# Attention scores of the first batch by single chunks on four row strips, in two lasting PSUM tiles, and the last stores on two queues

## Chip, cores, metric

One core of one Trainium2 chip. The metric is the device time of one execution in microseconds (us). The kernel before takes 404.97 us (median of 3 runs, 404.37 to 405.53). "Clock" below is the mean TensorE clock that was granted in a run, as a share of full speed.

## The reference

Attention over 8 batches of 12 heads (448 tokens, 64 wide), then a feed-forward layer with a SiLU gate on its result:

```python
def _attn_ref(q, k, v):                        # (8, 12, 448, 64) each
    scores = (1.0 / np.sqrt(64)) * np.matmul(q, k.transpose(0, 1, 3, 2))
    scores = scores - np.max(scores, axis=-1, keepdims=True)
    attn = np.exp(scores)
    attn = attn / (np.sum(attn, axis=-1, keepdims=True) + 1e-09)
    return np.matmul(attn, v)

def _moe_ref(x, w_in, w_out):                  # (3584, 768), (768, 2048), (2048, 768)
    h = x @ w_in
    g = h * (1.0 / (1.0 + np.exp(-h)))
    return g @ w_out
# ... x is the attention's result, heads side by side in each token's row
```

## The kernel before

The program is laid out by a small planner in Python that simulates the engines and emits each instruction when its inputs should be ready. Letters in the profile: **s** scores (TensorE), **E** their exponentials (ScalarE), **a** the sums and products with V (TensorE), **xT** the normalised attention, **h** the first feed-forward product, **th** its tanh, **G** the gated result (VectorE), **o** and **p** the second feed-forward product, **ost** results on their way out, **z** products of zeros whose only purpose is to keep TensorE going until the first h.

Batch 0 is cut into units of 224 queries (7 of the 14 blocks of 32), four heads and four chunks of keys each; the later batches have 448 queries. A score product has only 32 rows, and the program places the heads of a group in row strips of TensorE that work side by side: a group of eight products of 224 columns takes 0.60 us on two strips (kernel before, at 9.77 us). The program allots eight banks of PSUM (512 columns of FP32 each in its tiles): four for scores, four (tag "m") for everything else.

```python
def score_banks(n, w, ys):
    for y in ys:                               # y: heads 0,1 or heads 2,3
        pS_t[(n, w, y)] = ps.tile([128, 2, 512], FP32, name=f"s_{n}_{w}_{y}",
                                  tag="s", bufs=2)     # two banks per tile, two tiles

def per_burst(n):
    return 2 if units[n][0] == 0 else 1        # batch 0: two chunks to a tile

def scores(n, w, ys):
    score_banks(n, w, ys)
    for c in range(per_burst(n) * w, per_burst(n) * (w + 1)):
        for e in range(2):
            for y in ys:
                for h in (2 * y, 2 * y + 1):
                    score(pS_t[(n, w, y)], n, c, e, h, 0, rows_of(n, c) // 32, 0)

def expo(n, w, y):                             # ... one exponential per tile, 2 x 448 elements
    nc.scalar.activation(out=E[(n, w)][0:kr, 2*y : 2*y+2, 0:nk],
                         in_=pS_t[(n, w, y)][0:kr, :, 0:nk], func=AF.Exp, scale=attn_scale)
# ... in the planner
PACE = 3
s_ring = Ring(2)                               # free scores tiles
split = ((0,), (1,)) if ns[0] < 6 else ((0, 1),)   # batch 0: one tile (two heads) at a time
qk_seq += [(ns, c, ys) for c in range(NCH // per_burst(ns[0])) for ys in split]
# ... fill a gap of TensorE ahead of the first h; "wait" is the gap that the planner expects
n = max(1, int((wait - 0.06) / mm(128)))
od.on_pe(Op("PE", n * mm(128), lambda n=n: run_zeros(n)), "full")
# ... stores
eng = nc.scalar if w % 2 and 4 * qd + 4 == NT * B and i == j else nc.sync
```

The softmax here doesn't subtract the row's maximum and nothing guards it: scores larger than these inputs give would overflow.

## Time and profile before

| | before |
|---|---|
| time, median of 3 | 404.97 us |
| TensorE busy | 395.0 us of a span of 403.9 |
| ScalarE busy | 233.7 us |
| first s, first h, first s of batch 1 | 8.19, 23.66, 36.93 us |
| last product ends, last result ready, last store issued | 398.17, 398.76, 401.80 us |

Read the moments in the third row as follows: up to the first h the kernel waits for loads and exponentials, and TensorE's gaps are filled with z; from there TensorE is the bound (96% of the chain that ended last), so a delay of the first h reaches the end. Two groups of the page are needed for comparison: line, engine, operation, output and input, count, then busy time, mean ns of one, and the engine's idle time before them with what ended it.

```profile
L348 ACT ACTIVATE E<-s 128x896 f16<-128x896 f32 (+1 forms) x172 | 149.2, 915 | 48.8 <-PE s L311 47.5
L311 PE MATMUL s<-QT,KT 32*128 32x448 f16 (+4 forms) x864 | 56.4, 340 | 0.4 <-ACT E L348 0.4
```

TensorE's scores waited for ScalarE for 0.4 us in the whole run.

### The profile page before, as it was taken

Reading aid. Unit: us, or ns where it says so; the run is one execution under the profiler, and the core shown is the slowest. Engines: PE = TensorE matmul, PEld = TensorE weight load, DVE = VectorE, ACT = ScalarE, POOL = GpSimd, SP = SyncE. Lnnn points to the kernel's source line nnn. Section 1 sums busy time; section 2 is a strip of 40 time slices with the busy share of each in tenths; the row PEclk is TensorE's granted clock in tenths of the full one; section 3 lists DMA queues with packets and bytes.
Section 4 is the critical chain, followed back from the end, with each engine's and each line's share of the span. In section 5 each row is a group of like instructions: output and inputs, shape, how many; then the busy total and the mean of one; then the engine's idle time right before and its main releaser. Section 6 shows DMA issues by size and latency. Waiting matters only on the chain.

```text
span 403.9 us, 9442 instructions
## 1 busy us (share of the span) xinstructions
PE 395.0 (98%) x3767; PEld 203.7 (50%) x3767; DVE 299.3 (74%) x646; ACT 233.7 (58%) x360; POOL 95.9 (24%) x175
## 2 busy tenths in 40 slices
PE   8999999999999999999999999999999999999994
PEld 8676765444443444444445434444445444655562
DVE  2456686999979797696688578878697677674763
ACT  2887896696566866544961495664971573224410
POOL 6686383724003515120000630530000000000000
PEclk9999999999999999999999999999999999999999
DMA  7999999967014935392002782643001300131014
GB/s 106 158 151 206 204 136 213 200 94 116 2 39 99 173 56 71 64 177 56 0 2 58 123 142 44 92 81 68 0 21 47 94 0 2 35 81 44 2 49 107
DMA packets 38747, 34.43 MB, mean 85 GB/s; under 512 B 11952, under 2 KB 37936, under 8 KB 38704
## 3 DMA queue, kind: packets, MB, share of 16 engines
q0 software_dynamic: 27952, 22.82, 39.2%
q1 hardware_dynamic: 10560, 10.83, 10.4%
q8 instruction: 29, 0.48, 0.5%
q10 hardware_dynamic: 192, 0.20, 0.2%
q14 instruction: 14, 0.11, 0.1%
HBM read 45.61 MB, written 11.01 MB: 140 GB/s over the span
## 4 chain that ended last, share of the span: by engine, by line
PE 96%; DVE 1%; ACT 1%; issue 0%; ACTq 0%
PE h L446 37%; PE p L537 30%; PE s L311 12%; PE a L375 11%; PE o L551 3%; PE z L1148 2%; ACT E L348 1%; DVE T L359 1%; DVE rdn L424 0%; DVE ost L590 0%; DVE sT L415 0%; ACT ost L604 0%; DVE G L493 0%; DVE X L493 0%; DVE inv L421 0%
## 5 line engine op out<-in xcount | busy, mean ns | idle before, releaser
L348 ACT ACTIVATE E<-s 128x896 f16<-128x896 f32 (+1 forms) x172 | 149.2, 915 | 48.8 <-PE s L311 47.5
L446 PE MATMUL h<-xT,w_in_t 128*128 128x448 f16 (+1 forms) x864 | 157.8, 332 | 0.1
L446 PEld LDWEIGHTS <-w_in_t 128*128 128x128 f16 x864 | 79.2, 98 | 72.6 <-issue 19.4
L457 ACT ACTIVATE th<-h 128x448 f16<-128x448 f32 (+1 forms) x144 | 71.7, 505 | 58.1 <-PE h L446 53.5
L493 DVE SCALAR_TENSOR_TENSOR G<-th,h 128x448 f16<-128x448 f16 (+2 forms) x144 | 74.7, 532 | 35.2 <-ACT th L457 33.3
L250 POOL DMA_DIRECT2D V<-in_v_dram x88 | 48.6, 566 | 124.4 <-PE a L375 105.2
L311 PE MATMUL s<-QT,KT 32*128 32x448 f16 (+4 forms) x864 | 56.4, 340 | 0.4 <-ACT E L348 0.4
L537 PEld LDWEIGHTS <-G 128*128 128x128 f16 x384 | 36.7, 98 | 28.5 <-issue 4.6
L537 PEld LDWEIGHTS <-S 128*128 128x128 f16 x312 | 29.5, 98 | 22.8 <-issue 4.3
L375 PE MATMUL a<-E,V 128*32 128x448 f16 (+3 forms) x864 | 40.3, 334 | 0.5 <-issue 0.5
L537 PE MATMUL p<-D,G 128*128 128x384 f16 x208 | 37.8, 326 | 0.5 <-DVE sT L415 0.5
L537 PE MATMUL p<-w_out_t,S 128*128 128x384 f16 x208 | 36.8, 326 | 0.0
L432 DVE SCALAR_TENSOR_TENSOR xT<-a,rdn 128x448 f16<-128x448 f32 (+1 forms) x54 | 28.7, 560 | 6.7 <-PE a L375 6.2
L537 PE MATMUL p<-w_out_t,G 128*128 128x384 f16 x176 | 31.8, 326 | 0.0
L311 PEld LDWEIGHTS <-KT 32*128 32x128 f16 (+2 forms) x864 | 17.5, 98 | 27.9 <-issue 26.6
L359 DVE TENSOR_TENSOR T<-E,E 128x1792 f16<-128x1792 f16 x20 | 21.7, 1086 | 11.4 <-ACT E L348 11.4
L375 PEld LDWEIGHTS <-V 128*32 128x32 f16 (+2 forms) x864 | 18.2, 95 | 22.9 <-issue 15.3
L527 DVE TENSOR_TENSOR S<-G 128x512 f16<-128x512 f16 x70 | 26.5, 417 | 4.3 <-PE p L537 4.2
L359 DVE TENSOR_TENSOR T<-T,E 128x1792 f16<-128x1792 f16 x20 | 21.7, 1085 | 8.8 <-ACT E L348 8.8
L231 POOL DMA_DIRECT2D rk<-in_k_dram x24 | 13.7, 570 | 41.4 <-DVE KT L285 38.0
L285 DVE STREAM_TRANSPOSE KT<-rk 128x256 f32<-128x256 f32 (+3 forms) x48 | 16.6, 383 | 7.9 <-DMA rk<-in_k_dram 6.9
L600 ACT COPY ost<-p 128x384 f32<-128x384 f32 x13 | 6.3, 482 | 24.4 <-PE p L537 24.4
(41 smaller groups left out, 270.5 us busy)
## 6 DMA issues: line engine op xcount, KB each, us to landing
out_dram<-ost SPq DMA_DIRECT2D x220, 48.0 KB, 1.6
rk<-in_k_dram POOLq DMA_DIRECT2D x24, 224.0 KB, 5.1
rq<-in_q_dram POOLq DMA_DIRECT2D x21, 224.0 KB, 5.7
w_out_t<-in_moe_w_out_dram POOLq DMA_DIRECT2D x8, 384.0 KB, 8.9
V<-in_v_dram POOLq DMA_DIRECT2D x43, 64.0 KB, 4.5
V<-in_v_dram POOLq DMA_DIRECT2D x40, 48.0 KB, 4.2
w_in_t<-in_moe_w_in_dram POOLq DMA_DIRECT2D x16, 96.0 KB, 4.5
w_in_t<-in_moe_w_in_dram POOLq DMA_DIRECT2D x8, 192.0 KB, 7.9
```

The costliest lines, as they stand in the source:

```text
L250: nc.gpsimd.dma_start(out=VT[b][32 * x : 32 * (x + 1), hs, 0:count, :], in_=v[b, hs].rearrange("h (i g) d -> i h g d", g=TPP)[:, :, first ...
L285: nc.vector.transpose(out=turned.rearrange("p c x i -> p x c i")[:, x:y, 0:count], in_=t[:, first : first + count * (y - x)].rearrange("p ...
L311: nc.tensor.matmul(out=pS[p0 : p0 + 32 * (x1 - x0), h % 2, at : at + nq], lhsT=KT[(b, hg)][32 * h : 32 * (h + 1), c, x0:x1, :, e], rhs=QT[ ...
L348: nc.scalar.activation(out=E[(n, w)][0:kr, 2 * y : 2 * y + 2, 0:nk], in_=pS_t[(n, w, y)][0:kr, :, 0:nk], func=AF.Exp, scale=attn_scale,)
L359: nc.vector.tensor_tensor(out=T_t[n], in0=E[(n, 0)] if c == 1 else T_t[n], in1=E[(n, c)], op=ALU.add,)
L375: nc.tensor.matmul(out=a[32 * h : 32 * (h + 1), 0:nq], lhsT=w, rhs=e[k0:k1, h, at : at + nq], start=start, stop=stop,)
L432: nc.vector.scalar_tensor_tensor(out=xT[(b, cc)][:, 32 * g0 : 32 * g1], in0=acc[(n, part)][:, 0:nq], scalar=0.5, in1=rdn_t[n].rearrange("p ...
L446: nc.tensor.matmul(out=h[:, 0 : t1 - t0], lhsT=w_in_t[:, cc, 128 * f : 128 * (f + 1)], rhs=xT[(b, cc)][:, t0:t1], start=(cc == 0), stop=(c ...
L457: nc.scalar.activation(out=th, in_=h_t[(b, f, t0)][:, 0 : t1 - t0], func=AF.Tanh)
L493: nc.vector.scalar_tensor_tensor(out=dst[:, f, at + lo : at + hi], in0=th_t[(b, f, t0)][:, lo - t0 : hi - t0], scalar=1.0, in1=h_t[(b, f, ...
L527: nc.vector.tensor_tensor(out=dst[:, f0:f1], in0=x[:, f0:f1], in1=y[:, f0:f1], op=op)
L537: nc.tensor.matmul(out=pr_t[(qd, BANK[m])][:, 0:OH], lhsT=w[:, f, :], rhs=W_[m][:, f, :], start=(f == 0 and BANK[m] == m), stop=(f == HF - 1),
```

## The change

Intent: batch 0's score groups use all four row strips, chunk by chunk, and two tiles that last over the whole batch take the chunks alternately in their left and right column halves, so that one half can be read while the other is written. The planner is told that the halves are free of each other. With it come a new pace of the score groups and new priorities, and the last four outputs all use both store queues.

```diff
-    def score_banks(n, w, ys):
+    def score_banks(n, c, ys):
         for y in ys:
-            pS_t[(n, w, y)] = ps.tile([128, 2, 512], FP32, ..., tag="s", bufs=2)
+            key = y if units[n][0] == 0 else (n, c, y)
+            if key not in pS_t:
+                pS_t[key] = ps.tile([128, 2, 512], FP32, ..., tag="s", bufs=2)
+            pS_t[(n, c, y)] = pS_t[key]
 ...
-        for c in range(per_burst(n) * w, per_burst(n) * (w + 1)):
-            for e in range(2): ...
+        for e in range(2): ...               # one chunk; at = nq * (c % 2) picks the half
 ...
-            in_=pS_t[(n, w, y)][0:kr, :, 0:nk],
+            in_=pS_t[(n, c, y)][0:kr, :, at : at + nq],
 ...
-    s_ring = Ring(2)
+    s_ring = (Ring(2), Ring(2))              # one ring per half
 ...
-            split = ((0,), (1,)) if ns[0] < 6 else ((0, 1),)
-            qk_seq += [(ns, c, ys) for c in range(NCH // per_burst(ns[0])) for ys in split]
+            qk_seq += [(ns, c, (0, 1)) for c in range(NCH)]
 ...
-            eng = nc.scalar if w % 2 and 4 * qd + 4 == NT * B and i == j else nc.sync
+            eng = nc.scalar if w % 2 and 4 * qd + 4 == NT * B else nc.sync
 ...
-    PACE = 3
+    PACE = 3.8
 # priorities (bias): tanh -2 to -0.3, gate -1 to -4, combine_w 100 to 30, reads of results
 # -0.3/-1 to 0.5/0, add_e 0 to 2, inverse -10 to 0, norm -10 to -2; limits: od.now - 4 to
 # od.now - 2, len(moe) < 6 to len(moe) < 24
 # (cut: the same renaming from per_burst to per_tile elsewhere)
```

More of the change, by code (lines that the diff above doesn't have):

```diff
@@ L299, in turn_q @@
         QT[n] = qt
-    def score_banks(n, w, ys):
+    def score_banks(n, c, ys):
         for y in ys:
-            pS_t[(n, w, y)] = ps.tile(
-                [128, 2, 512], FP32, name=f"s_{n}_{w}_{y}", tag="s", bufs=2
-            )
+            key = y if units[n][0] == 0 else (n, c, y)
+            if key not in pS_t:
+                pS_t[key] = ps.tile([128, 2, 512], FP32, name=f"s_{n}_{c}_{y}", tag="s", bufs=2)
+            pS_t[(n, c, y)] = pS_t[key]
     def score(pS, n, c, e, h, x0, x1, p0):
@@ L309, in score @@
         nq = 32 * (g1 - g0)
-        at = nq * (c % per_burst(n))
+        at = nq * (c % per_tile(n))
         nc.tensor.matmul(
@@ L317, in score, with per_tile, scores @@
         )
-    def per_burst(n):
+    def per_tile(n):
         return 2 if units[n][0] == 0 else 1
-    def scores(n, w, ys):
-        score_banks(n, w, ys)
-        for c in range(per_burst(n) * w, per_burst(n) * (w + 1)):
-            for e in range(2):
-                for y in ys:
-                    for h in (2 * y, 2 * y + 1):
-                        score(pS_t[(n, w, y)], n, c, e, h, 0, rows_of(n, c) // 32, 0)
+    def scores(n, c, ys):
+        score_banks(n, c, ys)
+        for e in range(2):
+            for y in ys:
+                for h in (2 * y, 2 * y + 1):
+                    score(pS_t[(n, c, y)], n, c, e, h, 0, rows_of(n, c) // 32, 0)
     def scores_rest(n):
@@ L341, in rows_of, with expo @@
         return KROWS[c] if form(*units[n][:2]) == "lone" else 128
-    def expo(n, w, y):
-        kr = rows_of(n, w * per_burst(n))
-        nk = 32 * (units[n][3] - units[n][2]) * per_burst(n)
+    def expo(n, c, y):
+        kr = rows_of(n, c)
+        nq = 32 * (units[n][3] - units[n][2])
+        w, at = c // per_tile(n), nq * (c % per_tile(n))
         if (n, w) not in E:
@@ L348, in expo @@
         nc.scalar.activation(
-            out=E[(n, w)][0:kr, 2 * y : 2 * y + 2, 0:nk],
-            in_=pS_t[(n, w, y)][0:kr, :, 0:nk],
+            out=E[(n, w)][0:kr, 2 * y : 2 * y + 2, at : at + nq],
+            in_=pS_t[(n, c, y)][0:kr, :, at : at + nq],
             func=AF.Exp,
@@ L369, in attend_mm @@
         nq = 32 * (g1 - g0)
-        at = nq * (c % per_burst(n))
+        at = nq * (c % per_tile(n))
         if part == 0:
@@ L396, in attend @@
                     attend_mm(
-                        a, n, part, c, h, 0, rows_of(n, c), E[(n, c // per_burst(n))],
+                        a, n, part, c, h, 0, rows_of(n, c), E[(n, c // per_tile(n))],
                         c == 0, lone and c == NCH - 1,
@@ L631 @@
     od = Order()
-    s_ring, m_ring, e_ring = Ring(2), Ring(4), Ring(NE)
+    s_ring, m_ring, e_ring = (Ring(2), Ring(2)), Ring(4), Ring(NE)
     th_ring, tmp_ring, ost_ring = Ring(3), {3: Ring(2), 1: Ring(1)}, Ring(NOST)
@@ L750, in run @@
                 th = od.add(
-                    Op("ACT", act(t1 - t0), lambda: tanh(b, f, t0, t1), [op], -2, tail=0.2, ring=th_ring)
+                    Op("ACT", act(t1 - t0), lambda: tanh(b, f, t0, t1), [op], -0.3, tail=0.2, ring=th_ring)
                 )
@@ L757, in run @@
                     [th],
-                    -1,
+                    -4,
                     then=lambda at: (m_ring.give(at), th_ring.give(at)),
@@ L789, in sums_w @@
                         ld_wout[0] + ld_wout[1] + list(plain_op.values()) * (m in (3, 7)),
-                        100,
+                        30,
                     )
@@ L807, in run @@
                     [op],
-                    -0.3,
+                    0.5,
                     then=lambda at: (m_ring.give(at), ost_ring.give(at + STORED)),
@@ L864, in read @@
             busy = act(OH) if eng == "ACT" else OH / 960.0 + 0.13
-            bias = -0.3 if eng == "ACT" else -1
+            bias = 0.5 if eng == "ACT" else 0
             ring = tmp_ring[m] if m in tmp_ring else ost_ring if m in (2, 5, 6, 7) else None
@@ L985, in qk_at, with halves_of @@
         at = when([kt_op.get(units[n][:2]) for n in ns] + [qt_op.get(n) for n in ns])
-        s, e = s_ring.when(len(ys)), (e_ring.when(1) if ys[0] == 0 else 0.0)
-        if at is None or s is None or e is None:
-            return None
-        return max(at, s, e)
+        s = [r.when(len(ys)) for r in halves_of(n, c)]
+        e = e_ring.when(1) if c % per_tile(n) == 0 and ys[0] == 0 else 0.0
+        if at is None or None in s or e is None:
+            return None
+        return max(at, e, *s)
+    def halves_of(n, c):
+        return s_ring[c % 2 : c % 2 + 1] if units[n][0] == 0 else s_ring
     def run_qk():
@@ L994, in run_qk @@
         nq = 32 * (units[n][3] - units[n][2])
-        s_ring.take(len(ys))
-        if ys[0] == 0:
+        halves = halves_of(n, c)
+        for r in halves:
+            r.take(len(ys))
+        if c % per_tile(n) == 0 and ys[0] == 0:
             e_ring.take()
@@ L1000, in run_qk @@
             "PE",
-            2 * per_burst(n) * mm(nq) + (0.03 if rest else 0.013),
+            2 * mm(nq) + (0.03 if rest else 0.013),
             (lambda: scores_rest(n)) if rest else (lambda: scores(n, c, ys)),
@@ L1005, in run_qk @@
         op.half = len(ys) == 1
-        if c == NCH // per_burst(n) - 1 and ys[-1] == 1:
+        if c == NCH - 1 and ys[-1] == 1:
             done = []
@@ L1017, in run_qk @@
                     "ACT",
-                    act(2 * nq * per_burst(n)),
+                    act(2 * nq),
                     lambda y=y: expo(n, c, y),
@@ L1021, in run_qk @@
                     tail=0.2,
-                    then=s_ring.give,
+                    then=lambda at: [r.give(at) for r in halves],
                 )
@@ L1039, in plan_e @@
             t_op[n] = [
-                od.add(Op("DVE", HG * S / 1920.0 + 0.1, lambda n=n, c=c: add_e(n, c), deps, 0))
+                od.add(Op("DVE", HG * S / 1920.0 + 0.1, lambda n=n, c=c: add_e(n, c), deps, 2))
             ]
@@ L1060, in av_at @@
         for n in ns:
-            if len(exp_op.get(n, ())) < 2 * NCH // per_burst(n):
+            if len(exp_op.get(n, ())) < 2 * NCH:
                 return None
@@ L1064, in av_at @@
             for i, x in enumerate(exp_op[n]):
-                c = i // 2 * per_burst(n)
+                c = i // 2
                 if len(ns) == 2 and c == NCH - 1:
@@ L1096, in then @@
             def then(at):
-                for _ in range(7 if two else NCH // per_burst(ns[0])):
+                for _ in range(7 if two else NCH // per_tile(ns[0])):
                     e_ring.give(at)
@@ L1119, in after_av @@
                     made[-1:] + before[step],
-                    -10,
+                    0,
                 )
@@ L1131, in after_av @@
                 [op] + rdn_op[n],
-                -10,
+                -2,
                 then=m_ring.give,
@@ L1167 @@
             if qk is not None and qk <= od.now and (
-                od.now >= pace["next"] or moe_i is None or len(moe) < 6
+                od.now >= pace["next"] or moe_i is None or len(moe) < 24
             ):
                 u0 = units[qk_seq[0][0][0]]
-                pace["next"] = min(max(pace["next"], od.now - 4), od.now) + PACE * len(qk_seq[0][2]) / 2
+                pace["next"] = min(max(pace["next"], od.now - 2), od.now) + PACE * len(qk_seq[0][2]) / 2
                 run_qk()
```

## The prediction

> **What bounds the kernel now.** I read the page first (busy time, clock row, chain), then TensorE's waits, then the timeline of the first 45 us and of the last 20.
>
> ```profile
> PE 395.0 (98%) x3767; PEld 203.7 (50%) x3767; DVE 299.3 (74%) x646; ACT 233.7 (58%) x360; POOL 95.9 (24%) x175
> ...
> PEclk9999999999999999999999999999999999999999
> ...
> PE 96%; DVE 1%; ACT 1%; issue 0%; ACTq 0%
> ```
>
> TensorE is busy throughout at full clock and is 96% of the chain. Its own list of waits is nearly empty:
>
> ```profile
> PE z L1148 <- DVE zeros L214: 1.0, 1, 1.0
> PE a L375 <- ACT E L348: 0.6, 1, 0.6
> PE p L537 <- DVE sT L415: 0.5, 1, 0.5
> PE a L375 <- issue: 0.5, 1, 0.5
> PE s L311 <- ACT E L348: 0.4, 1, 0.4
> ```
>
> But busy is not useful everywhere: until the first h, TensorE fills gaps with products of zeros (z). The timeline of the start and of the first scores of batch 1:
>
> ```profile
> 8.19 0.60 PE L311 MATMUL s<-QT,KT 32*128 32x224 f16 x16
> ...
> 8.80 4.14 ACT L348 ACTIVATE E<-s 128x896 f16<-128x896 f32 x5 [6.78 <-PE s L311]
> ...
> 9.77 0.60 PE L311 MATMUL s<-QT,KT 32*96 32x224 f16 x8 [0.43 <-ACT E L348]
> ...
> 23.66 0.74 PE L446 MATMUL h<-xT,w_in_t 128*128 128x224 f16 x6
> ...
> 36.93 0.58 PE L311 MATMUL s<-QT,KT 32*128 32x448 f16 x8
> ...
> 37.54 1.73 ACT L348 ACTIVATE E<-s 128x896 f16<-128x896 f32 x2 [0.96 <-PE s L311]
> ```
>
> So there are two regimes. From 8.2 to 23.66 the exponentials on ScalarE pace the kernel: five stand back to back in 4.14 us, a step of (4.14-0.915)/4 = 0.81 us each. From 23.66 on TensorE does, and everything that delays the first h delays the end. The end is a third regime, stores:
>
> ```profile
> 385.71 16.09 SPq L585 DMA_DIRECT2D out_dram<-ost  x28
> ...
> 397.98 1.82 ACTq L585 DMA_DIRECT2D out_dram<-ost  x4
> 398.20 0.56 DVE L590 TENSOR_TENSOR ost<-p,s 128x384 f32<-128x384 f32 x1 [0.26 <-PE p L537]
> ```
>
> The last result is ready at 398.76, but SyncE's queue still works through its stores to 385.71+16.09 = 401.80; the span ends 2.1 us later.
>
> [...]
>
> **The change part by part.**
>
> *Scores of batch 0.* Both kernels issue 24 groups of 8 products of 224 columns. Before, a group is two chunks of two heads, two row strips at a time: [...]the timeline has 0.50 to 0.53 from such a group to the next. After, it is one chunk of four heads on four strips[...]. [...]17 of the 24 groups stand before the first h (16 before the change), where TensorE waits anyway.
>
> *Exponentials of batch 0.* 24 of 896 elements become 48 of 448. Steps of 0.81 us at 896 and 0.237 at 224 (tanh) give about 0.43 at 448, so 0.85 for a pair: only 0.05 us more per chunk.
>
> *The banks.* This is where I choose. The four scores banks now belong to two tiles that last over the batch, and chunks alternate between their column halves. The kernel's own planner counts the halves as free of each other. The waits in the built program say otherwise[...]. In unit 0, the third chunk's first product waits for the exponential of chunk 2, heads 0 and 1, which reads the other half; the exponential of chunk 2, heads 2 and 3, waits for the third chunk's last product; and so on through the batch. Elsewhere the products wait for both exponentials of the chunk just before. Two engines that had two buffers now take turns. One turn:
> - two exponentials, the first 0.43 to the next's start, the second to its end 0.546 (the tanh row of that size): 0.97;
> - from an exponential's end to the waiting product: 0.05 (9.72 to 9.77 before);
> - from the first product to the start of the exponential: at 36.93/37.54, 0.61 us[...].
>
> Sum 1.45 us per chunk, against 0.81 for the same elements before. The first exponential still starts at 8.80. The third chunk's products come at 8.80 + 2x0.43 + 0.546 + 0.05 = 10.25, the seventeenth 14 turns later at 30.55, and the first h follows 0.32 us on, at **30.9 instead of 23.66: +7.2 us**. V's arrival (16.7), which held a 0.46 us wait before, no longer matters.
>
> From there to batch 1's first scores I walked the two engines through the remaining 7 chunks, the 7 h and the products with V in the built order. [...]the turns go on: with one h (0.56 us) between two chunks TensorE is back before the exponential is done, waits of 0.44, 0.55, 0.39, 0.3 and 0.65 us, 2.3 in sum. Before, this stretch had 1.0 in all, mostly the 0.6 of the list. Batch 1's scores come at about 43.5 instead of 36.93; one h fewer is done by then (0.56) and 16 products with V more (0.19), so the lag is **+6.9 us**. Everything after is TensorE's work without slack, so this lag reaches the end.
>
> *Pace and priorities.* The work from there is the same. Counting changes of mode in the built order: 180 against 185, -0.6 us. Waits left there in the trace before, as excess over the usual steps, add to about 4 us; the new order may gain or lose part of them, which I put at zero.
>
> *Stores.* Four of the 20 stores that SyncE issues after 392.2 go to ScalarE: 4 x 0.48 = 1.9 us off the backlog. The last pair of each queue can start only after 398.76 and needs some 0.9, so both queues end near 399.9, with a little for waits between stores: **-1.8 us**.
>
> Sum: 404.97 + 6.9 - 0.6 - 1.8 = **409.5 us**, 1.1% slower.
>
> **Rivals.**
> 1. *The turns cost nothing, the halves work as planned.* Then chunks flow at 0.85 us, the first h comes about 1 us earlier, 1.7 us are saved after it and 1.8 at the end: about 400.5. For it: the change was built around that; the kernel before shows five exponentials without a gap. Against it: the waits are in the built program, one engine's product on the other's exponential in every chunk, and no other work is there to fill the gaps.
> 2. *The turns cost more*, because the idle turns make TensorE's clock drop, or because a turn has hand-over times that I read too short. At half the clock a chunk gains 0.19 us and everything near it doubles: 3 to 4 us more, 413. For it: in each turn TensorE streams scores for 0.19 us and zeros for about 0.3 of 1.45 us.[...]
> 3. *The new order of the rest takes back the loss.* At most the 4 us of leftover waits: 405.5. It can also lose some: the normalisations and reads of results lose priority on VectorE, and later x or late banks would stall TensorE.
>
> **Range and chances.** The turn time carries the sum: 0.1 us per turn is 1.4 us at the first h. With plus or minus 1.5 us for that, 2 for the order of the rest and 0.5 for the end, 8 in 10 is **405.5 to 413.0**. Faster by over 2% would be below 396.9, which even rival 1 does not reach: 0.01. Slower by over 2% is above 413.1 and needs rival 2 or a bad order: 0.09. Within 2%: 0.90.
>
> **What would show it right or wrong.** In the timeline after: exponentials of 448 elements in pairs with idle time of about 0.5 us after every second, ended by PE s; the third chunk's products near 10.25; first h near 30.9 (rival 1: about 22.7); batch 1's first scores near 43.5. In the waits: PE s waiting for ACT E, several times with about 2 us in all after the first h. In the groups: exponentials of 448 at about 0.55 each. At the end: before, the last store's issue ends 3.0 us after the last result is ready (398.76 to 401.80); I expect 1.1 to 1.3, on both queues. If the first h is near 23 the lockstep is refuted; if it is near 31 and the total is below 405, the later order gained what I put at zero.

The sum came to 409.5 us, as printed; these of its terms lost their figures:

- The streaming times of a score group on two strips and on four are cut, and with them the third term of the turn, put at 0.43 us, and the 1.7 us that TensorE was to save from the first h to batch 1's scores. By the traces, a group on four strips takes 0.41 us and one on two 0.60, which is 0.19 less. With that, the third term is 0.61 - 0.19 = 0.42 us and the turn 0.97 + 0.05 + 0.42 = 1.44. Products of h of 224 columns follow each other at 0.097 us (trace before); an estimate from that for the saving, 8 x 4 x 0.097 - 7 x 2 x 0.097, is again 1.7 us.
- The cost of a change of mode (the next products are of another shape), from which the -0.6 us for five changes fewer comes, is cut. In the trace before, six products of h take 0.67 us from their start to the scores' (23.66 to 24.33), twelve 1.25 (27.82 to 29.07): 0.097 us each and 0.09 for the change, so five changes would be 0.45 us.
- The 0.48 us of a store, from one issue to the next, stood in a cut paragraph and is read from the trace before: there SyncE's issues in the backlog start 0.36 to 0.52 us apart, 0.46 in the mean (eight from 392.21 to 395.87).

One h (0.56 us) is 0.58 us by the same lines of the trace; 16 products with V (0.19) are 0.39 (32 take 0.96 us, 16 take 0.57); with both, the lag of 6.9 us would be 6.8.

## The result, and the profile after

The changed kernel takes **415.62 us** (median of 4 runs: 415.48, 414.11, 415.76, 416.03; clock 0.977 to 0.985), against 405.08 (4 runs) for the kernel before in the same rounds: **ratio 1.0255, 95% interval 1.0225 to 1.0285, slower**. A ratio here is the mean time of one kernel's fast runs over that of the other's fast runs of the same rounds, so it is not quite the ratio of the quoted medians. "Fast" means within 1.5% of the kernel's own fastest run. A kernel that loses clock in every run has only such runs, so I give the clock beside the times.

Parts 1, 2 and 5 of the page of the kernel after (busy times; the granted clock in 40 slices of 10.3 us, in tenths; the same two groups as before):

```profile
PE 399.8 (97%) x3794; PEld 205.7 (50%) x3794; DVE 299.9 (73%) x646; ACT 237.1 (57%) x384; POOL 95.8 (23%) x175
...
PEclk9578999999999999999999999999999999999998
...
L350 ACT ACTIVATE E<-s 128x896 f16<-128x896 f32 (+3 forms) x196 | 150.9, 822 | 58.5 <-PE s L312 57.8
...
L312 PE MATMUL s<-QT,KT 32*128 32x448 f16 (+4 forms) x864 | 55.6, 350 | 6.8 <-ACT E L350 6.2
```

Work barely changed: 1.7 us more on ScalarE for 24 more exponentials, 0.8 us less on scores. Three other things did. Scores wait for E 6.2 us instead of 0.4; ScalarE sits idle before its exponentials 58.5 us instead of 48.8; and the clock row, 9s throughout before, has a dip to 5, 7 and 8 in its second to fourth slices.

The timeline of the kernel after, first turns (start, duration, engine, instruction, count, idle time before it and what ended that):

```profile
8.05 1.42 ACT L350 ACTIVATE E<-s 128x448 f16<-128x448 f32 x3 [6.03 <-PE s L312]
9.51 0.41 PE L312 MATMUL s<-QT,KT 32*96 32x224 f16 x8 [0.78 <-ACT E L350]
9.85 0.51 PE L1155 MATMUL z<-zeros 128*128 128x128 f16 x6
9.97 0.97 ACT L350 ACTIVATE E<-s 128x448 f16<-128x448 f32 x2 [0.50 <-PE s L312]
10.99 0.41 PE L312 MATMUL s<-QT,KT 32*96 32x224 f16 x8 [0.63 <-ACT E L350]
...
16.11 0.61 PE L312 MATMUL s<-QT,KT 32*96 32x224 f16 x8 [0.75 <-ACT E L350]
...
17.80 0.61 PE L312 MATMUL s<-QT,KT 32*96 32x224 f16 x8 [0.32 <-ACT E L350]
...
32.84 1.30 PE L448 MATMUL h<-xT,w_in_t 128*128 128x224 f16 x6
...
46.31 0.57 PE L312 MATMUL s<-QT,KT 32*128 32x448 f16 x8
```

TensorE and ScalarE take turns: each score group waits for an exponential, each pair of exponentials waits for a score group. A turn lasts 10.99 - 9.51 = 1.48 us, later 17.80 - 16.11 = 1.69. The later turns are longer because TensorE's part is: 0.61 us for the same eight products instead of 0.41. The windows of both kernels (length, busy time and count of PE, PEld, DVE, ACT, POOL, then the granted clock, DMA share, GB/s), before first:

```profile
10.00:15.00 5.00, 5.00 (x82) 3.33 (x79) 2.15 (x6) 4.78 (x7) 2.38 (x5) 1.00 1.30 160
```

after:

```profile
10.00:15.00 5.00, 3.74 (x58) 2.12 (x57) 1.52 (x4) 2.88 (x6) 2.87 (x6) 0.72 1.29 160
15.00:20.00 5.00, 3.72 (x44) 2.35 (x41) 0.62 (x3) 2.92 (x6) 4.50 (x9) 0.50 1.19 186
20.00:25.00 5.00, 5.00 (x93) 3.12 (x93) 2.45 (x7) 3.10 (x7) 3.86 (x7) 0.50 0.99 149
```

From about 12 us to about 26 TensorE ran at half clock, and for a few us more between 30 and 40 (0.77 and 0.89 in the windows 30 to 35 and 35 to 40). Everything on the way to the first h is affected. Note that "PE busy" is 5.00 in the last window although the engine runs at half speed: the busy column alone hides this, the clock column shows it.

Cutting both profiled runs at the same five moments shows where the time went. "Again" is the same changed kernel; the last two columns are experiments described below (both at a clock of 0.998 in these runs):

| stretch, us | before | after | after, again | more zeros | turns alone |
|---|---|---|---|---|---|
| start to first s | 8.19 | 7.44 | 8.15 | 7.28 | 7.32 |
| first s to first h | 15.47 | 25.40 | 22.50 | 22.90 | 22.92 |
| first h to first s of batch 1 | 13.27 | 13.47 | 13.57 | 12.95 | 12.91 |
| from there to the last product's end | 361.24 | 362.56 | 362.56 | 362.55 | 362.28 |
| from there to the end of the span | 5.76 | 4.84 | 4.99 | 4.05 | 3.93 |
| span | 403.93 | 413.71 | 411.77 | 409.73 | 409.36 |

The first row is not the change's doing: over all profiled runs of all variants it lies between 6.67 and 8.19. The second row carries +9.9 us, the fourth +1.3, the fifth -0.9.

### The profile page after: what moved, and what is told of

Same layout as the page of the kernel before. It is cut to its first block, busy times and chain, and to the rows that moved or that the text cites. A ratio compares the mean times of both kernels' runs of the same rounds, so it can differ in the third digit from the quotient of the medians.

```text
span 413.7 us, 9524 instructions
## 1 busy us (share of the span) xinstructions
PE 399.8 (97%) x3794; PEld 205.7 (50%) x3794; DVE 299.9 (73%) x646; ACT 237.1 (57%) x384; POOL 95.8 (23%) x175
## 4 chain that ended last, share of the span: by engine, by line
PE 93%; ACT 4%; DVE 1%; issue 0%
PE h L448 36%; PE p L539 29%; PE a L377 12%; PE s L312 12%; ACT E L350 4%; PE o L553 3%; PE z L1155 2%; DVE G L495 0%; DVE T L361 0%; DVE QT L296 0%; DVE ost L592 0%; ACT th L459 0%; DVE inv L423 0%; DVE zeros L214 0%; DVE ones L212 0%
## 5 line engine op out<-in xcount | busy, mean ns | idle before, releaser
L350 ACT ACTIVATE E<-s 128x896 f16<-128x896 f32 (+3 forms) x196 | 150.9, 822 | 58.5 <-PE s L312 57.8
L448 PEld LDWEIGHTS <-w_in_t 128*128 128x128 f16 x864 | 80.6, 98 | 70.3 <-issue 15.1
L377 PE MATMUL a<-E,V 128*32 128x448 f16 (+3 forms) x864 | 42.6, 346 | 0.7 <-DVE G L495 0.7
L539 PEld LDWEIGHTS <-S 128*128 128x128 f16 x312 | 29.4, 98 | 22.9 <-issue 4.5
L312 PEld LDWEIGHTS <-KT 32*128 32x128 f16 (+2 forms) x864 | 15.4, 100 | 35.5 <-issue 33.0
L377 PEld LDWEIGHTS <-V 128*32 128x32 f16 (+2 forms) x864 | 19.2, 99 | 24.3 <-issue 16.3
L417 DVE STREAM_TRANSPOSE sT<-a 128x448 f32<-128x448 f32 (+1 forms) x27 | 15.7, 582 | 11.3 <-PE a L377 10.7
```

What stands on the lines that cost most here:

```text
L312: nc.tensor.matmul(out=pS[p0 : p0 + 32 * (x1 - x0), h % 2, at : at + nq], lhsT=KT[(b, hg)][32 * h : 32 * (h + 1), c, x0:x1, :, e], rhs=QT[ ...
L350: nc.scalar.activation(out=E[(n, w)][0:kr, 2 * y : 2 * y + 2, at : at + nq], in_=pS_t[(n, c, y)][0:kr, :, at : at + nq], func=AF.Exp, scal ...
L377: nc.tensor.matmul(out=a[32 * h : 32 * (h + 1), 0:nq], lhsT=w, rhs=e[k0:k1, h, at : at + nq], start=start, stop=stop,)
L448: nc.tensor.matmul(out=h[:, 0 : t1 - t0], lhsT=w_in_t[:, cc, 128 * f : 128 * (f + 1)], rhs=xT[(b, cc)][:, t0:t1], start=(cc == 0), stop=(c ...
L539: nc.tensor.matmul(out=pr_t[(qd, BANK[m])][:, 0:OH], lhsT=w[:, f, :], rhs=W_[m][:, f, :], start=(f == 0 and BANK[m] == m), stop=(f == HF - 1),
```

## The experiments

Each is built from one of the two kernels. All gave results that agree with the reference. The first four ran on one chip, beside ten runs of the kernel before (median 405.27; two of the ten were slow: 410.93 and 411.09, clock 0.986 and 0.977).

### Old scores, everything else new

The kernel after, with batch 0's scores as before (the score hunks and `s_ring` of the diff undone).

> The changed kernel with batch 0's scores, exponentials and scores tiles as before (two chunks of two heads, 24 exponentials of 896); pace, priorities and stores stay changed. If the lasting, shared banks cost the time (theory A), the first h is back near 23.7 us, the clock stays full and the total is within 2 us of the kernel before less the 0.9 us at the end: 402 to 406 us. If pace and priorities cost it (theory B), the first h may be near 23.7 but the total stays above 410.

Measured: 404.99 us, **ratio 0.9993** (0.9979 to 1.0008), clock 0.998 to 1.000; first h at 22.94. So the loss is in the scores: without them pace, priorities and stores together change nothing.

### The scores alone

The kernel before with only the score hunks and `s_ring` of the diff.

> The kernel before with only the scores of batch 0 changed; pace, priorities and stores of before. Theory A: first h near 32 to 33 us as in the changed kernel, total 413 to 418. Theory B (pace and priorities): close to 405.

Measured: 415.72 us, **ratio 1.0271** (1.0243 to 1.0299), clock 0.975 to 0.987; first h at 32.56. The scores' change alone gives the whole loss, 10.5 us.

### The stores alone

```diff
-            eng = nc.scalar if w % 2 and 4 * qd + 4 == NT * B and i == j else nc.sync
+            eng = nc.scalar if w % 2 and 4 * qd + 4 == NT * B else nc.sync
```

> The kernel before with only the stores of the last four outputs on two queues. My prediction's term: 1.8 us less (403.2). The trace of the changed kernel, whose end after the last product is 4.84 us against 5.76, says 0.9 us less (404.1). If the end is bound by the last transfers and not by the queue, no change.

Measured: 403.27 us, **ratio 0.9948** (0.9934 to 0.9962), five of the six runs between 403.08 and 403.33. This is the best kernel and beats both, by 2.0 us and 12. From the last result to the end of the last store's issue it takes 1.3 us, 3.04 before. Its profile fell in its one disturbed run (408.10 us, clock 0.987), which is read only for that end.

The three results also show what pace and priorities cost by themselves: old scores, with them, 404.99; stores alone, without them, 403.27. That is **+1.7 us**.

### More zeros in each gap

The kernel after, its order untouched, with six more products of zeros in the first filled gap after each score group (210 instead of 138). This tests whether the clock, not the turns, made the difference between 409.5 and 415.6.

```diff
     def scores(n, c, ys):
+        warm["s"] = 1
 ...
-        for _ in range(n):
+        for _ in range(n + 6 * warm.pop("s", 0)):
             nc.tensor.matmul(out=warm["z"][:, 0:128], lhsT=zeros, rhs=zeros, ...)
```

> The changed kernel with six more products of zeros (0.33 us) in each of the gaps that zeros fill in the first 33 us, the order otherwise the same. If the halved clock between about 12 and 26 us adds to the turns (theory C), the granted clock stays at 1.00 there, a turn goes from 1.65 to 1.47 us, and the first h comes 1.5 to 2.5 us earlier, near 30.7; total 412 to 414. If the zeros delay the scores, or the clock falls all the same, no gain or a loss.

Measured: 411.65 us, **ratio 1.0162** (1.0147 to 1.0177), clock 0.995 to 0.998. Timeline and one of the windows of this kernel:

```profile
9.36 0.41 PE L314 MATMUL s<-QT,KT 32*96 32x224 f16 x8 [0.45 <-ACT E L353]
9.69 0.84 PE L1156 MATMUL z<-zeros 128*128 128x128 f16 x12
10.83 0.41 PE L314 MATMUL s<-QT,KT 32*96 32x224 f16 x8 [0.29 <-ACT E L353]
```

```profile
15.00:20.00 5.00, 4.17 (x78) 3.10 (x78) 0.15 (x2) 3.51 (x8) 4.46 (x8) 1.00 1.21 191
```

A turn is still 10.83 - 9.36 = 1.47 us, but the clock stays at 1.00 and no turn grows. Adding work to TensorE made the kernel 3 to 4 us faster (1.0162 against 1.0255, or against 1.0237 in the second submission below); in the profiled runs up to 0.9 us of that lies at the end of the span, in the stores (fifth row of the table), so the clock's own share is some 2 to 3 us. What is left, 22.90 us from first s to first h, is the turns by themselves: the prediction has 30.9 - 8.19 = 22.7.

### Two chunks on four strips, fresh tiles

A second set ran on another chip, beside twelve runs of the kernel before (median 405.07). The first asks whether the lasting tiles and halves are needed for the loss, or four strips suffice. The kernel before, with one group for both tiles:

```diff
-            split = ((0,), (1,)) if ns[0] < 6 else ((0, 1),)
+            split = ((0, 1),)
```

> The kernel before with its scores groups of batch 0 (two chunks, exponentials of 896, fresh tiles) made for all four heads at once on four strips, as a group of 16 products. The turn theory, from the same three terms: [...]two exponentials 0.81 + 0.915, hand-over 0.05: a group of two chunks every 2.4 us, 1.2 us per chunk, between 0.81 of before and 1.45 to 1.65 of the change; first h about 16 us after the first scores. If it is the shared halves or the chunking alone that cost time and four strips are free (rival), the exponentials stand back to back at 0.81 as before.

(The first of the three terms is the 0.61 us from the first product to the exponential, at 36.93 and 37.54 us in the trace before.)

Measured: 409.54 us, **ratio 1.0109** (1.0095 to 1.0123), clock 0.992 to 0.999. Its timeline:

```profile
8.24 1.73 ACT L348 ACTIVATE E<-s 128x896 f16<-128x896 f32 x2 [6.22 <-PE s L311]
...
10.57 1.72 ACT L348 ACTIVATE E<-s 96x896 f16<-96x896 f32 x2 [0.60 <-PE s L311]
```

The turn is there too: 2.33 us for two chunks, with 0.60 us of ScalarE idle, where nothing else stands between the groups (0.96 to 1.88 us idle where sums or products with V do). Here no halves exist, only groups that write all four scores banks. So the turn comes with writing all four banks by one group, and cutting it into single chunks makes it cost twice as often: 1.17 us per chunk here, 1.48 in the changed kernel, 0.81 before.

### Single chunks in halves, two strips

The converse: lasting tiles, halves and single chunks stay, but a group again writes only one tile.

```diff
-            qk_seq += [(ns, c, (0, 1)) for c in range(NCH)]
+            split = ((0,), (1,)) if ns[0] < 6 else ((0, 1),)
+            qk_seq += [(ns, c, ys) for c in range(NCH) for ys in split]
```

> The changed kernel with each chunk made in two groups of two heads on two strips, still 48 exponentials of 448 in the halves of lasting tiles. The turn theory: TensorE can write one tile's banks while ScalarE reads the other's; a tile's own turn is [...]1.02 us per chunk, against 1.45 with four strips at full clock; total 3 to 6 us below the changed kernel. If lasting tiles or small exponentials are what costs time (rival), the turn stays near 1.45 and the total near 415.

(The terms of the 1.02 us are 0.546 + 0.05 + 0.42.)

Measured: 424.76 us, **ratio 1.0487** (1.0471 to 1.0504), clock 0.961 to 0.962. As a prediction of the time this failed; the mechanism that it was built to show is in its timeline and windows:

```profile
8.13 3.07 ACT L350 ACTIVATE E<-s 128x448 f16<-128x448 f32 x6 [0.50 <-PE s L312]
...
8.73 0.40 PE L312 MATMUL s<-QT,KT 32*96 32x224 f16 x4
...
9.76 0.40 PE L312 MATMUL s<-QT,KT 32*96 32x224 f16 x4
```

```profile
10.00:15.00 5.00, 4.47 (x53) 2.12 (x49) 2.08 (x6) 3.70 (x8) 2.26 (x5) 0.56 1.31 161
```

While the clock is full, six exponentials stand in a row with no wait long enough for the view to show (at 0.54 us each, one every (3.07 - 0.54)/5 = 0.51 us; the two of a pair above are 0.97 - 0.54 = 0.43 apart), and a chunk takes 9.76 - 8.73 = 1.03 us, close to the 1.02 that was expected of a tile's own turn. Then the clock falls (0.50 in each five-us window from 15 to 30 us) and the later order, planned anew, has a stretch of score groups waiting for ScalarE at 135 to 142 us, where the clock dips once more. So two strips undo the turn over all four banks: 1.03 us per chunk instead of 1.48. They don't bring back the 0.81 of before, so the lasting tiles with single chunks keep a smaller cost of their own. This run says nothing about what two strips would be worth at full clock.

### Two attempts at a steadier version

Both add to the stores-alone kernel, in whose profile the clock dip (0.79 in the window 15 to 20 us, 0.50 from 20 to 25) follows a wait for V of 1.56 us at 16.58. The first makes the planner expect V of batch 0 later:

```diff
-            mb = MB * (hg1 - hg0) * X_TOK[form(b, hg0)][x][1]
+            mb = (1.5 if b == 0 else 1) * MB * (hg1 - hg0) * X_TOK[form(b, hg0)][x][1]
```

> A version meant to beat both: the kernel before, the stores on two queues, and batch 0's V taken by the planner to arrive later, so that two more scores groups stand ahead of the first products with V. The 1.4 us gap in the exponentials at 17.3 us should go: 0.5 to 1.5 us less than with the stores alone (403.3), so about 402.3; and no dip of the clock there, so no run near 408 or 411.

Measured: 405.65 us, ratio 1.0013 (1.0001 to 1.0025); one of seven runs slow (414.42, clock 0.969). That run is the profiled one: its clock falls at about 11.6 us (0.66 in the window 10 to 15 us), before any product with V, and no gap of TensorE between the first scores and there is above 0.43 us (busy 1.57 us from 8 to 10 us and 5.00 from 10 to 15). No gain, and behind the stores alone (0.9948, on another chip).

The second puts 16 products of zeros before the first products with V (`run_zeros(16)` after the bank of the first such product is made):

> The kernel before, the stores on two queues, and 16 products of zeros (0.9 us) ahead of the first products with V, where TensorE otherwise idles for V. If idleness there causes the slow runs of the kernel before (2 of 10 near 411, and one of 6 near 408 with the stores alone), no run lies above 405; the fast runs are within 0.5 us of 403.3. If the dips come from elsewhere, they stay.

Measured: 404.71 us, ratio 0.9998 (0.9969 to 1.0028); its six runs go from 403.56 to 408.32 (clock 0.987). The dip was not prevented. Both failed as improvements.

### The turns alone at full clock

A third set, on a third chip, with seven runs of the kernel before (median 405.42; two slow, 411.01 and 410.95, clock 0.977). This kernel has the new scores with the extra zeros and the new stores, but the old pace and priorities.

> The scores of the change at full clock (six more zeros per gap), the stores on two queues, but pace and priorities as before. Against the stores alone it leaves only the turns: my sum's +6.9 us, so 403.3 + 6.9 = 410.2, with the clock at 1.00 and the first h near 30. Against the same with the changed pace and priorities (411.65) it should be about 1.5 us less, as old scores with and without them differ by 1.7. If the turns cost less than I think, below 408.

Measured: 411.35 us, **ratio 1.0158** (1.0140 to 1.0175), clock 0.998 to 0.999. Against the stores alone (0.9948) the turns cost 0.0210, about 8.1 to 8.5 us, at full clock. Against the kernel with more zeros (1.0162) the difference is within the noise: with these scores the new pace and priorities cost nothing measurable, though they cost 1.7 us with the old ones. The two effects do not simply add.

### No zeros at all

The stores-alone kernel without any product of zeros after the first scores. If the clock follows how much TensorE streams, and not the turns, it must fall here too, in the order of the kernel before.

```diff
-        for _ in range(n):
+        for _ in range(0 if S_seen else n):       # S_seen is filled by the first scores
```

> The kernel before with the stores on two queues, and without the products of zeros after the first scores; order otherwise the same. If a TensorE that streams for too small a share of the time loses its clock even where no single gap is long, the clock is at 0.5 for 10 us or more in the first 30, in every run, and the total is 3 to 8 us above 403.3. If only a gap of over 1.5 us does it (as in the slow runs), most runs stay at 403.3.

Measured: 409.12 us (407.95 to 409.52, all four runs at a clock of 0.977 to 0.979), **ratio 1.0097** (1.0072 to 1.0121): 5.9 us more than with the zeros (403.27, on another chip). Its windows:

```profile
10.00:15.00 5.00, 4.32 (x56) 2.76 (x56) 1.91 (x6) 4.21 (x6) 2.60 (x5) 0.62 1.34 165
15.00:20.00 5.00, 4.83 (x80) 3.25 (x79) 2.54 (x7) 2.43 (x4) 4.77 (x9) 0.50 1.21 192
```

The same dip as in the changed kernel, without its scores. Before the dip the longest gap of TensorE after its first scores is 0.99 us; the 1.5 us of the expectation came from the wait of 1.56 us in the profile of the stores alone.

### The changed kernel again

> The changed kernel unaltered, on the same chip as the two others, so that the clock's share is read in one set: 415.6 as before; less 411.65 for more zeros, the clock's share is 4 us. Its end after the last product was 4.84 us in the one profile, against 4.05 in the runs with the same stores; if that was chance, it is 4.0 to 4.1 here.

Measured: 414.34 us, **ratio 1.0237** (1.0213 to 1.0261); runs and clocks 413.55 (0.993), 414.02 (0.981), 414.66 (0.980), 415.13 (0.976). Lower clock goes with longer time, in this order. Both expectations were missed: the time is 2.7 us above that of more zeros (on another chip) instead of 4, and the end after the last product is 4.99 us instead of 4.0 to 4.1. The profiled run is the first, and in it the clock held through the turns and fell only late:

```profile
15.00:20.00 5.00, 2.94 (x58) 2.11 (x60) 0.57 (x2) 3.46 (x8) 4.48 (x9) 1.00 1.15 180
...
30.00:35.00 5.00, 4.67 (x80) 2.97 (x80) 1.55 (x6) 2.95 (x8) 2.93 (x5) 0.66 1.08 196
```

That run gives the turns of the unaltered changed kernel at full clock: 22.50 us from first s to first h, +7.0 over before. Against it, the first run's 25.40 has 2.9 us of clock.

## Why the prediction was wrong, point by point

It said 409.5 us, between 405.5 and 413.0; it is 415.62. By its own sum, measured on the profiled runs:

| term | predicted | measured |
|---|---|---|
| turns, to the first h | +7.2 | +7.0 (again), +7.4 (more zeros, turns alone) |
| first h to batch 1's scores | -0.65 | -0.3 (more zeros), -0.4 (turns alone) |
| everything after, to the last product | +0.4 - 0.6 = -0.2 | +1.3 (changed kernel and more zeros), +1.0 (turns alone) |
| stores | -1.8 | -1.7 to -1.8 (more zeros, turns alone), -0.9 and -0.8 (changed kernel) |
| clock | 0 | +2.9 and +0.5, first two terms of the first profile; -0.75 is the earlier start of that run |

**The turns: right.** Third chunk at 9.51, 1.46 us after the first exponential's start (8.05); predicted 10.25 - 8.80 = 1.45. Every pair of exponentials is followed by about 0.5 us of idle time ended by PE s, as stated. First h minus first s: 22.5 to 22.9 at full clock, predicted 22.7. Rival 1 (halves work as planned, 400.5) is refuted by the first turn. Two readings behind the sum were slightly off, without effect on it. Its streaming time rested on a figure that no trace here shows; in the trace before, products of h of 224 columns follow each other at 0.097 us (24 take 2.41 us, 18 take 1.83). And TensorE was not "at full clock" throughout: up to about 7 us the zeros of 128 columns start 0.107 us apart, later 0.056. The clock column reads 1.00 there only because the records of the clock begin at 6.95 us.

**The clock: the step that failed.** The sum had it at zero. It cost 3.4 us in the first profile and some 2 to 3 us by the kernel with more zeros, the largest part of the 6.1 us between 409.5 and 415.62; two other terms were mis-sized, the later waits by 1.5 us and the end by 0.9 (below). Rival 2 was priced well ("3 to 4 us more, 413"; 3.4 in the first profile; at clock 0.50 a score group took 0.61 us instead of 0.41 and six products of h 1.30 instead of 0.75), but it was set aside because the gaps are short, and slower by over 2% got 0.09. The length of the gaps was the wrong test. At full clock a turn of the changed kernel streams, by an estimate with the 0.097 us per 224 columns of h, 2 x 0.097 us of scores and 6 products of zeros at 0.055 us each (twelve take 0.84 us, six 0.51): 0.52 of 1.48 us, 35%. With 12 zeros it is 0.85 us, 58%. The kernel before, with two or three zeros in a group's 0.81 us, has (4 x 0.097 + 0.11 to 0.17)/0.81, 61 to 69%; without zeros 48%. Of all runs, those with 35% (12 runs) have clocks of 0.975 to 0.993, those with 48% (no zeros, 4 runs) 0.977 to 0.979, and those with 58% (8 runs) 0.995 to 0.999. The longest gap in the changed kernel's turns before its clock fell is 0.78 us.

That the clock is higher with zeros is shown by two one-sided changes, one in each direction (with more of them 0.995 to 0.998 instead of 0.975 to 0.993; without any 0.977 to 0.979, and 0.998 to 1.000 with them in five of the six runs of the stores alone); the exact rule is not. A share alone does not decide it: in the profiled run of the second submission the same 35% kept the full clock until 30 us. And the kernel before, at 61 to 69%, loses it in 5 of its 33 runs (409.5 to 411.1 us, clock 0.977 to 0.986); the version with a later V, whose scores are those of before, lost it with no gap above 0.43 us. By the clock of the windows of five us, taken as 0.50 in a dip, the dips in the first 40 us last 13.7 and 3.4 us (changed kernel; 0.50 from 12.21 to 25.86 and from 32.69 to 36.10), 3.4 (again), 10.2 and 6.8 (scores alone) and 17 (no zeros). What starts and what ends one, no run shows. The cause of the low share is the planner: it fills the gap that it expects, and it believed the halves independent, so it put 6 zeros where the real turn had room for 12.

**Pace and priorities: put at -0.6, in fact not a gain.** The changes of mode came out as counted (180 in the trace after, 185 before), but the waits did not stay the same: from batch 1's first scores on, TensorE's list of waits has 2.6 us, 0.5 before. The stretch grew by less, 1.3 us, so other steps took some of that back. These lines of the timeline after show the three largest:

```profile
68.44 0.94 PE L377 MATMUL a<-E,V 128*32 128x448 f16 x16 [0.73 <-DVE G L495]
69.60 0.57 PE L312 MATMUL s<-QT,KT 32*128 32x448 f16 x8 [0.21 <-DVE QT L296]
...
76.03 0.57 PE L312 MATMUL s<-QT,KT 32*128 32x448 f16 x8
77.60 0.40 PE L312 MATMUL s<-QT,KT 32*64 32x448 f16 x4 [1.00 <-ACT E L350]
78.41 0.60 PE L312 MATMUL s<-QT,KT 32*64 32x448 f16 x12 [0.41 <-ACT E L350]
```

A bank of h was freed late (0.73), and a third score group followed two others before ScalarE was done with them (1.00 and 0.41). The kernel with old pace and priorities has other waits of nearly the same sum (2.2; 362.28 us in the fourth row instead of 362.56), and the scores alone give 362.29. So some 1.0 of the 1.3 us comes with the new scores and not with pace and priorities. That the cause is the shifted start, for which the planner's times no longer fit, is argued and not shown; rival 3 named that it could lose, and the sum had it at zero.

**Stores: right where they are undisturbed.** -2.0 us alone (predicted -1.8), and 1.3 us from last result to last issue (predicted 1.1 to 1.3). In the changed kernel that end was 2.1 and 2.3 us. One line of the store's instructions in the last 12 us tells why (min/median/max of an issue in ns); the kernel after first, the kernel with more zeros second:

```profile
L587 SPq DMA_DIRECT2D out_dram<-ost x16: 315/419/1618, 402.9 to 411.2; - x16
```

```profile
L590 SPq DMA_DIRECT2D out_dram<-ost x16: 314/419/429, 399.7 to 407.3; - x16
```

One issue of 1.62 us (1.26 in the second submission, 1.60 in the scores alone) instead of 0.42, in the backlog at the end where nothing absorbs it. The trace before has eleven issues of 0.62 to 1.64 us on SyncE among 220, the trace after five of 1.29 to 1.95 among 216; in these three runs a long one fell into the last 12 us (in turns alone one of 0.79 us did no visible harm). What makes an issue slow, and whether it falls there in every run of the changed kernel, is open.

Together: 4.5 predicted, with +3.4 of clock, +1.5 of later waits, +0.9 of store issue, +0.2 of turns and -0.75 of start this is the 9.8 us between the two profiled spans.

## What to carry to other kernels

Look at whether one group of products writes all the banks that its consumer reads. Here it did, and the exponentials waited for the products and the products for them: 0.19 us saved per group on TensorE's four strips cost a turn of 1.48 us per chunk instead of 0.81. With two tiles in banks of their own, written by two strips each, the engines overlapped (0.81 us per chunk before, with five exponentials back to back in 4.14 us; 1.03 in lasting halves). A planner has to model the unit by which the program really waits, here not the column half: a chunk's products waited for exponentials of the other half (0.78 us up to 9.51 in the trace after, where the third exponential, of the second chunk, ends at 8.05 + 1.42 = 9.47). Each exponential reads both banks of its tile, so no run tells bank and tile apart. When gaps are filled to hold the clock, size the filling by the real gap: the longer turn with the filling planned for a short one cost twice here, 7.0 us in waiting and 2.9 in clock (second row of the table, again and first profile); and read the clock column, because busy time does not show it (5.00 of 5.00 us at clock 0.50, window 20 to 25).
